# A backward pass on one core: when the first turned pieces of w1 and the row buffer are set up

## The chip, the cores and the metric

The kernel runs on one core of a Trainium2 chip. The metric is the device time of one execution in microseconds; three executions of the kernel before gave 1100.77, 1101.2 and 1102.52.

The core has five engines with instruction streams of their own: PE (TensorE, matrix products; its weight loads are listed as PEld), DVE (VectorE), ACT (ScalarE), POOL (GpSimd) and SP (SyncE, which only issues loads here). Semaphores order them. Data comes from HBM into SBUF by DMA transfers.

## The reference

Two rows (a batch of 2, one token each, width 1024) go through attention, an MLP, the same attention and the same MLP again, each with a layer norm ahead of it and added to the residual. The kernel returns the result and the gradients of everything in it for a given gradient of the output.

```python
x = x + A(layernorm(x), k_cache, v_cache, wq, wo)   # layer 0: 32 heads, 4 KV heads, 16384 keys, width 128
x = x + B(layernorm(x), w1, b1, w2, b2)             # 1024 -> 3584 -> 1024, gelu
x = x + A(layernorm(x), k_cache, v_cache, wq, wo)   # layer 1: the same weights and caches
x = x + B(layernorm(x), w1, b1, w2, b2)
# returned: x, and by vjp with grad_out the gradients of x, k_cache, v_cache, wq, wo, w1, b1, w2, b2
```

The caches are 33.6 MB each for K and V, and they are read from HBM in every attention, forward and backward, but for some pieces that are kept from one pass to the next. The gradients that are written have the size of what they belong to.

## The kernel before, in words

**A program of steps, and a planner.** The kernel doesn't issue instructions as it is read. `emit(fn, uses)` (L71) appends a step to a list; `uses` names the chunks (pieces of data of up to 1 MB, [128, 4096] bfloat16) that the step touches. At the end `Program.run` (L109) goes through the list in order, gives each chunk a home (one of the buffers that the profile calls `slot`, `late`, `e` and `ds`) and calls the steps, which then issue instructions. The order on each engine is thus the order of `emit`.

A chunk with a load is fetched by a DMA on SP's queue (L378 for K and V, L383 for rows of weights). Loads are taken in the order of first use. Before each step the planner hands out homes for the next loads as long as it can: a home must be free, it must not be given up before the chunk's last use, and `possible` (L124) must find that every later chunk still gets a home in time, the chunks without a load (turned copies, the row buffer) included. Of the homes that fit, `fit` takes the one that is given up first. A load whose home was used by others waits, in SP's queue, until their last readers are done; the loads behind it wait too. A chunk without a load gets its home at its first step.

Around the change there are 17 homes of 1 MB. Nine last to the end. Eight are given up for staging outputs later on: three at the mark "late", the others in the course of the next stage (marks 4, 8, 12, 16 and 18, L23 and L24, L1612).

**Turned pieces.** A product with a transposed weight needs the weight turned. For w1, `turn_rows` (L436) does it on DVE: two 32x32 transposes (L442) turn one loaded piece into a turned copy, a chunk of its own, t, which `turned_products` (L484, matmuls at L492) then uses. w1 comes here in eight pieces, 0 to 7 (`ws1c`), of 896 KB; piece 7 is turned already from earlier in the program. So there are 14 turns, `t1[0]` to `t1[13]`, two for each of the pieces 0 to 6, and eight groups of products, `p1[0]` to `p1[7]`. A loaded piece's home is free after its second turn, a turned copy's after its products. w2 was turned in place earlier (`turn_here`) and lies in seven groups, 0 to 6; `here_products` (L466, matmuls at L470) uses it four rows j at a time, 32 matmuls for a group.

**The place of the change** is the passage from the backward attention of layer 1 to that of layer 0. `attn_bwd(1, ...)` (L1048) ends with `after`, then `tail` (the products with the last wq, at L470, eight steps), then `parts` (the layer norm's backward: sums at L672 to L677, closing at L683, rest at L690 to L693, which gives gM_all). Before the change `after` is `t1[0:1]`. Then come: the zeroing of the row buffer Y on ACT (L1533; Y holds rows that the products of weight gradients read later, and lasts to the end), `t1[1:3]`, the products of w2 with gM_all for j = 0 to 27 with one turn behind each of the first three groups, the step `dh0_` (L1543, and the spread at L511 and L512), the mark "late", the step that puts the first rows into Y (`y_rows`, L1300 and L1301), `t1[6:8]`, and the products `p1` with a unit of the weight gradients of w2 (`dw_units`, L1337) and the remaining turns between them:

```python
for n, b in enumerate(p1):
    emit(*b)
    for u in first[n + 1:n + 2] + t1[8 + n + max(0, n - 5):9 + n + max(0, n - 4)]:
        emit(*u)
```

Behind them stands the layer norm's backward of the MLP (L540 to L693), the products with wo (L470), the spread of the result, and the first block of layer 0's attention: `kblock` (L548), which turns a part of a V piece on DVE (L554) and multiplies on PE (L567). Its outputs, the gradients of K and V, are cast by ACT and DVE (L276, L279) and written by POOL's queue (L1287); the weight gradients are written at L1367.

Of the kernel before, what the change touches and what calls it, by code (L numbers as in the profile page):

```python
# [10 lines left out]
I32 = mybir.dt.int32  # L11
# [46 lines left out]
class Program:  # L58
# [12 lines left out]
    def emit(self, fn, uses=()):  # L71
        i = len(self.ops)
        self.ops.append((fn, tuple(uses)))
        for c in uses:
            if c.first is None:
                c.first = i
            c.last = i
# [105 lines left out]
def kernel(  # L183
# [26 lines left out]
    S = nc.scalar  # L210
# [16 lines left out]
    CH = 4096  # L227

    P = Program()
    emit = P.emit  # L230
# [66 lines left out]
    for w in range(2):  # L297
        for e in range(2):
            V.tensor_copy(out=selp[:, 2 * w + e],
                          in_=ident[:].rearrange("p (w t e) -> p w e t", w=2, e=2)[:, w, e].unsqueeze(1).to_broadcast(  # L300
                              [128, 4, 32]))
# [38 lines left out]
    wide = {}  # L340
# [23 lines left out]
    saved = {}  # L364
# [101 lines left out]
    def here_products(c, off, n, ps, v, fresh=True):  # L466

        def fn():
            for o in range(n):
                PE.matmul(ps(), lhsT=c.ap[:, off + o * 128:off + (o + 1) * 128], rhs=v(o),  # L470
                          start=(fresh and o == 0), stop=(o == n - 1), skip_group_check=True)

        return fn, [c]
# [152 lines left out]
    def col_to_row(colT, dram_out, queue=None, kind="half"):  # L626
        c = P.chunk(kind=kind)

        def f():
            row = c.ap[0:DJ, 0:256].rearrange("p (b n) -> p b n", b=2)  # L630
            ps = ob()[0:DJ, 0:256].rearrange("p (b n) -> p b n", b=2)
            for b in range(2):
                PE.transpose(ps[:, b, :], colT[:, :, b], identf[:])
            V.tensor_copy(out=row, in_=ps)
            (queue or GP).dma_start(dram_out.rearrange("b (j n) -> j b n", n=128), row)

        return f, [c]
# [352 lines left out]
    def wo_first_ops(l, k, ws=None):  # L990

        ws = ld_wo(k) if ws is None else ws
        ps = sb[0][:, 64:80].rearrange("p (r b) -> p r b", b=2)
        turns = [turn_here(ws[r // 4], (r % 4) * 1024, 8) for r in range(R)]
        prods = [here_products(ws[r // 4], (r % 4) * 1024, 8, lambda r=r: ps[:, r, :],
                               lambda o: gA_all[:, o, 2 * l:2 * l + 2]) for r in range(R)]
        return ws, turns, prods + [(lambda: do_of(l, k, ps), ())]
# [41 lines left out]
    def wq_last_ops(l, k):  # L1039

        ws = ld_wq(k)
        ps = sb[0][:, 112:128].rearrange("p (j b) -> p j b", b=2)
        turns = [turn_here(ws[j // 4], (j % 4) * 1024, 8, "act" if l == 1 else None) for j in range(DJ)]
        prods = [here_products(ws[j // 4], (j % 4) * 1024, 8, lambda j=j: ps[:, j, :],
                               lambda r: dq_all[:, k * R + r, 2 * l:2 * l + 2], l == 0) for j in range(DJ)]
        return turns, prods

    def attn_bwd(l, order, gT, wo_first, outputs=None, mark=None, extra=None, after=()):  # L1048

        kvs = []  # L1050
        for g in order:
# [40 lines left out]
        for pos, g in enumerate(order):  # L1092
            quick = l == 0 and pos == G - 1
            for f in range(2):
                n = 117 + 5 * f if quick else 16 * pos + 10 + 8 * f
# [9 lines left out]
        tail = []  # L1105
        for i, k in enumerate(kvs):
# [16 lines left out]
            else:  # L1123
                if l == 0:
                    wb.setdefault(32 * i + 12 + LAG_B, []).append((dn_kept, ()))
                ops, tail = wq_last_ops(l, k)
# [11 lines left out]
        while s <= n_steps:  # L1138
# [16 lines left out]
            n = -(-len(fill) // 3)  # L1155
            for fn, us in pre:
                emit(fn, us)
            between = fill[:n] + mids + fill[n:2 * n]
            for v in v_at.get(s, ()):
# [4 lines left out]
                between = []  # L1164
# [9 lines left out]
        aflush()  # L1174
        parts = attn_in_bwd(l, gT, dnq)
        if l == 1:
            todo = list(after) + tail + parts
        else:
            rows, kv_units, units = outputs(s, True)
            todo = ev.pop(s) + kv_units[0:4] + rows + kv_units[4:6] + tail[0:4] + kv_units[6:8] + tail[4:] + kv_units[8:10]  # L1180
            todo += parts[0:1] + units[0:4] + parts[1:2] + units[4:8] + parts[2:3] + kv_units[10:15] + parts[3:]
            todo += kv_units[15:] + units[8:]
# [4 lines left out]
    def attn_in_bwd(l, gT, dnq):  # L1187
        h = {}

        def sums():  # L1190
            last = sb[0][:, 112:128].rearrange("p (j b) -> p j b", b=2)
            if l == 0:
                dn = wrk.tile([128, DJ, 2], F32, name="dn")
                V.tensor_tensor(out=dn[:], in0=last, in1=dnq[:], op=ALU.add)
                last = dn[:]
            h["dr"], h["s"], h["g"] = ln_bwd_terms(last, vec_y[f"a{l}"][:], vec_r[f"a{l}"][:], gT()[:])
            dve(0.8)

        def close():
            h["ps"] = ln_bwd_sums(h["dr"], h["s"], h["g"], half[0, 0] if l == 1 else sb[0][:, 200:])  # L1200

        def rest():
            gn = saved[f"gA{l}"]
            ln_bwd_rest(h["ps"], h["dr"], vec_y[f"a{l}"][:], ([gM_all[:, :, 0:2]] if l == 1 else []) + [gn[:]])
            dve(0.8)

        res = [(sums, ()), (close, ()), (rest, ())]
        if l == 0:
            res.append(col_to_row(saved["gA0"], out_1.rearrange("b s d -> (b s) d"), nc.sync))
        return res  # L1210
# [82 lines left out]
    Y = P.chunk()  # L1293

    def y_rows(colT, j0, jn, q, at_):

        def f():
            tp = ob().bitcast(BF16)[32 * q:32 * q + 4, 0:jn * 128].rearrange("p (a b) -> p a b", b=128)
            for j in range(jn):
                PE.transpose(tp[:, j, :], colT[:, j0 + j, :], ident[:])  # L1300
            S.copy(out=Y.ap[32 * q:32 * q + 4, at_:at_ + jn * 128], in_=flat(tp))  # L1301
            load_of("act", 0.7)

        return f, [Y]
# [105 lines left out]
    up = [b * HKV + k for k in range(HKV) for b in range(2)]  # L1410
# [3 lines left out]
    def mark(name):  # L1414
        def f(n=0):
            marks[name, n] = len(P.ops)
        return f
# [61 lines left out]
    ws_o, wo_turns1, wo_prods = wo_first_ops(1, up[0] % HKV)  # L1479
# [28 lines left out]
    extra = {2: [(lambda: V.memset(fps1, 0.0), ())]}  # L1508
# [13 lines left out]
    t1, p1 = [], []  # L1522
    for n, c in enumerate(ws1c):
        t = w1t[n // 4][n % 4] if n == 7 else P.chunk()
        t1 += [] if n == 7 else turn_rows(c, t, 896)
        p1 += turned_products(lambda n=n: dm_0[:, n // 4], t, 14 * (n % 4), 14, vh0, n % 4 == 0, n % 4 == 3)
    extra[111] = [col_to_row(xM1, out_0.rearrange("b s d -> (b s) d"), kind="load")]
    attn_bwd(1, up, lambda: saved["g3"], (None, wo_prods), mark=mark("d1"), extra=extra, after=t1[0:1])
    wo_prods0 = wo_first_ops(0, down[0] % HKV, saved["wo"])[2]


    g2 = saved["gA1"]
    emit(lambda: S.copy(out=Y.ap.bitcast(I32), in_=wide["n"][:, 0:2].bitcast(I32).to_broadcast([128, CH // 2])), [Y])  # L1533
    for b in t1[1:3]:
        emit(*b)
    for j in range(FJ):
        emit(*here_products(ws2c[j // 4], (j % 4) * 1024, 8, lambda j=j: dhps0[:, j, :],
                            lambda o: gM_all[:, o, 0:2]))
        if j % 4 == 3 and j < 12:
            emit(*t1[3 + j // 4])  # L1540

    def dh0_():
        V.scalar_tensor_tensor(out=dh_all[:, :, 0:2], in0=dhps0, scalar=-1.0, in1=saved["nslope0"][:], op0=ALU.mult,  # L1543
# [6 lines left out]
    emit(lambda: load_of("dve", 6.0))  # L1550
    first = [y_rows(gM_all, 0, 8, 0, 0)] + dw_units("h", 0, 0, pieces_rows(out_8, F, D))
    rest_h = first[15:]
    for b in first[0:1] + t1[6:8]:
        emit(*b)
    for n, b in enumerate(p1):
        emit(*b)
# [10 lines left out]
    extra = {4: [(spread_a0, ())]}  # L1567
# [22 lines left out]
    def outputs(s, rest=False):  # L1590
        if rest:
            fin = late.pop(s)
            return fin[0:1], sum([sched.pop(x) for x in sorted(sched)], []), bg + fin[1:]
        if s in STAGE:
            mark(s)()
        if s in (68, 78):
            mark("done")(s // 78)
        res = list(sched.pop(s, ()))
        if s in late:
            bg.extend(late.pop(s))  # L1600
        if s >= 5:
            state["credit"] += 0.5 if s < 24 else max(1.3, len(bg) / (120 - s)) if s < 116 else 3
        while bg and state["credit"] >= 1:
            res.append(bg.pop(0))
            state["credit"] -= 1
        state["credit"] = min(state["credit"], 2.0)
        return res

    attn_bwd(0, down, lambda: saved["g1"], (va0, wo_prods0), outputs=outputs, extra=extra)
    slots = []  # L1610
    for i, t in enumerate(slot_tiles):
# [46 lines left out]
```

## Time and profile before

| | |
|---|---|
| median of 3 runs | 1101.2 us (1100.77 to 1102.52) |
| the profiled execution | 1101.63 us, span 1099.9 us, mean granted PE clock 0.829 |
| busy: PE, PEld, DVE, ACT, POOL | 820.7, 609.9, 753.9, 487.3, 176.3 us |
| DMA | 448.07 MB, 407 GB/s over the span |
| HBM | 347.23 MB read, 98.62 MB written |

The span runs from the first to the last instruction of the program; the execution's time has a little more around it. The profile also gives the busy share of the 16 DMA engines and the clock that PE was granted, in any stretch. In the rows of the timeline the columns are start, duration, engine, line, operation, what it writes and reads, shapes, how many, and in brackets how long the engine was idle ahead of it and what ended that. A row can merge several instructions of one kind that follow each other; for SP its duration is from the first issue to the last.

### The profile page before, as it was taken

The page shows a single profiled execution, that of the slowest core. Times are in us where ns is not written, and L with a number is a line of the kernel's source. Part 1 is how long each engine was busy: PE and PEld are TensorE (multiplying, and loading weights), DVE is VectorE, ACT ScalarE, POOL GpSimd, SP SyncE. Part 2 cuts the span into 40 slices and gives each one's busy share as a digit, 9 for nine tenths or more (in the row PEclk, how much of TensorE's full clock was granted, in tenths as well). Part 3 has the DMA queues.
Part 4 walks back from the last instruction along what each step waited for, and adds up shares of the span by engine and source line. Part 5 has one row for each costly group of instructions (what it writes and reads, how often), then busy time and mean ns, then how long its engine had stood idle before and what let it go on. Part 6 is the DMA issues. An engine that isn't in the chain of part 4 may idle for free. (4 is left out here: it accounts for less than half of the span.)

```text
span 1099.9 us, 34167 instructions
## 1 busy us (share of the span) xinstructions
PE 820.7 (75%) x14717; PEld 609.9 (55%) x14717; DVE 753.9 (69%) x1442; ACT 487.3 (44%) x1101; POOL 176.3 (16%) x550
## 2 busy tenths in 40 slices
PE   5665666457788657788877678988787788887886
PEld 4554565456777547687877574544443344443453
DVE  5864665168888727765745465978786779786985
ACT  0332222101242321235534326777675667675874
POOL 1000000001000000111211111332332333333330
PEclk9999999999555555579767757989997899898998
DMA  9999999999999999999999999999999999999996
GB/s 368 420 423 420 421 425 422 398 394 408 419 421 421 421 422 378 413 418 420 416 422 403 367 362 415 357 422 423 420 402 425 422 420 415 424 422 422 414 423 269
DMA packets 97404, 448.07 MB, mean 407 GB/s; under 512 B 7608, under 2 KB 11214, under 8 KB 58852
## 3 DMA queue, kind: packets, MB, share of 16 engines
q1 hardware_dynamic: 80004, 350.40, 78.3%
q0 software_dynamic: 17248, 95.48, 21.0%
q8 instruction: 115, 1.88, 0.6%
q14 instruction: 37, 0.30, 0.1%
HBM read 347.23 MB, written 98.62 MB: 405 GB/s over the span
## 5 line engine op out<-in xcount | busy, mean ns | idle before, releaser
L554 DVE STREAM_TRANSPOSE kT<-slot 128x512 int32<-128x512 int32 x432 | 291.7, 695 | 114.5 <-PE sc L567 91.3
L567 PE MATMUL sc<-qbd,kT 128*128 128x32 bf16 x4096 | 263.8, 223 | 13.0 <-DVE kT L554 10.3
L567 PEld LDWEIGHTS <-kT 128*128 128x128 bf16 x4096 | 209.1, 115 | 53.4 <-issue 21.7
L592 PEld LDWEIGHTS <-slot 128*128 128x128 bf16 x3424 | 141.0, 103 | 105.8 <-issue 54.9
L276 ACT CAST slot<-sc 128x512 bf16<-128x512 f32 x294 | 167.3, 592 | 65.2 <-PE sc L1337 29.8
L592 PE MATMUL sb<-xt,slot 128*128 128x8 bf16 x3424 | 156.8, 177 | 41.8 <-DMA slot<-in_A_v_cache_dram 24.1
L1277 PE MATMUL sc<-slot,late 128*128 128x512 bf16 x358 | 135.6, 403 | 29.7 <-DVE slot L279 11.5
L279 DVE CAST slot<-sc 128x512 bf16<-128x512 f32 x163 | 109.3, 677 | 35.8 <-PE sc L1277 15.5
L787 ACT ACTIVATE e<-sc 128x512 bf16<-128x512 f32 x32 | 19.0, 597 | 235.3 <-DVE sc L784 168.5
L460 ACT COPY slot<-tp 128x512 int32<-128x512 int32 x92 | 52.5, 586 | 113.8 <-PE tp L457 93.5
L276 ACT CAST slot<-sb 128x512 bf16<-128x512 f32 x135 | 80.1, 593 | 33.5 <-PE sb L1277 12.5
L457 PE MATMUL tp<-ident,slot 128*128 128x128 bf16 x800 | 75.7, 256 | 14.0 <-DMA slot<-in_A_wq_dram 8.1
L1277 PEld LDWEIGHTS <-late 128*128 128x128 bf16 x512 | 44.4, 99 | 63.6 <-issue 51.2
L602 ACT COPY xt<-e 32x128 int32<-32x128 int32 x256 | 75.6, 295 | 3.9
L1277 PE MATMUL sb<-slot,late 128*128 128x512 bf16 x154 | 62.5, 406 | 16.6 <-ACT slot L276 5.9
L279 DVE CAST slot<-sb 128x512 bf16<-128x512 f32 x92 | 62.5, 679 | 16.5 <-PE sb L1277 7.6
L457 PEld LDWEIGHTS <-slot 128*128 128x128 bf16 x800 | 61.3, 117 | 17.0 <-DMA slot<-in_A_wq_dram 8.5
L1337 PE MATMUL sc<-slot,late 128*128 128x512 bf16 x151 | 60.5, 419 | 4.2 <-DVE slot L279 1.5
L602 POOL COPY xt<-ds 32x64 int32<-32x64 int32 x128 | 29.5, 231 | 180.6 <-DVE ds L1070 107.1
L602 POOL COPY xt<-late 32x64 int32<-32x64 int32 x240 | 55.2, 230 | 15.0 <-DVE late L1070 2.3
L662 POOL TENSOR_TENSOR m_rstd<-ln_vpe,neghalf 128x2 f32<-128x2 f32 x2 | 1.4, 718 | 349.5 <-DVE ln_vpe L660 349.5
L442 DVE STREAM_TRANSPOSE slot<-slot 128x1024 int32<-128x1024 int32 (+1 forms) x44 | 50.9, 1182 | 1.0 <-DMA slot<-in_B_w_dram 0.9
(291 smaller groups left out, 1083.3 us busy)
## 6 DMA issues: line engine op xcount, KB each, us to landing
slot<-in_A_k_cache_dram SPq DMA_DIRECT2D x102, 1024.0 KB, 15.4
slot<-in_A_v_cache_dram SPq DMA_DIRECT2D x100, 1024.0 KB, 17.0
out_dram<-slot POOLq DMA_DIRECT2D x55, 1024.0 KB, 15.8
slot<-in_A_wq_dram SPq DMA_DIRECT2D x26, 1024.0 KB, 15.5
slot<-in_A_wo_dram SPq DMA_DIRECT2D x25, 1024.0 KB, 18.3
out_dram<-slot POOLq DMA_DIRECT2D x40, 512.0 KB, 16.6
slot<-in_B_w_dram SPq DMA_DIRECT2D x21, 896.0 KB, 15.7
slot<-in_B_w_dram SPq DMA_DIRECT2D x12, 1024.0 KB, 13.4
```

The source lines that it names most:

```text
L276: S.copy(out=dst, in_=src)
L279: V.tensor_copy(out=dst, in_=src)
L442: V.transpose(out=t.ap[:, h * nw * 256:(h + 1) * nw * 256].bitcast(I32).rearrange("p (w j m) -> p w j m", j=4, m=32), in_=c.ap[:, 0:4 * nc ...
L457: PE.transpose(tp[:, j * 128:(j + 1) * 128], c.ap[:, off + j * 128:off + (j + 1) * 128], ident[:])
L460: S.copy(out=d.bitcast(I32), in_=tp.bitcast(I32))
L554: V.transpose(out=kT[:].bitcast(I32).rearrange("p (w j m) -> p w j m", w=4, j=4), in_=c.ap[:, (i % 4) * 1024:(i % 4 + 1) * 1024].bitcast(I ...
L567: PE.matmul(sc[:, a0:a0 + 4, :, 2 * (i % 4) + q], lhsT=kv[:, 2 * q + w, :, e], rhs=qbd[:, q_at(g), 2 * w + e], start=(w == 0 and e == 0), ...
L592: PE.matmul(acc, lhsT=c.ap[:, n * 128:(n + 1) * 128], rhs=xv[:, i // 4, t // 2, :, 2 * (i % 4) + t % 2], start=(fresh and i == 0 and t == ...
L602: (GP.tensor_copy if on[t % len(on)] == "g" else S.copy)(out=d[32 * t:32 * t + 32, c0:c0 + cn, j, :], in_=s[32 * j:32 * j + 32, c0:c0 + cn ...
L787: S.activation(out=e_of(l, g)[:, 8 * f:8 * f + 8].rearrange("p a h b -> p h a b"), in_=sc[f][:].rearrange("p h (a b) -> p h a b", b=8), fu ...
L1277: PE.matmul(ps, lhsT=hold["blk"][:, j, :], rhs=flat(qm(w)[:, hf * 4:hf * 4 + 4, :]), start=True, stop=True)
L1337: PE.matmul(ps, lhsT=hold[j // 4 * 4][:, j % 4, :], rhs=Y.ap[:, y_at + c0:y_at + c0 + cn], start=True, stop=True)
```

## The change

Only the order of steps changes. The first turn leaves the end of `attn_bwd(1, ...)`, and the parameter `after` goes with it. The zeroing of Y and the first turns stand behind groups of w2's products: both turns of piece 0 behind group 0, the zeroing and the first turn of piece 1 behind group 1, the second turn of piece 1 behind group 2, the first of piece 2 behind group 3. The second turn of piece 2 moves behind `dh0_` and the step of Y's first rows, ahead of the two turns of piece 3.

```diff
-    def attn_bwd(l, order, gT, wo_first, outputs=None, mark=None, extra=None, after=()):
+    def attn_bwd(l, order, gT, wo_first, outputs=None, mark=None, extra=None):
...
         if l == 1:
-            todo = list(after) + tail + parts
+            todo = tail + parts
...
-    attn_bwd(1, up, lambda: saved["g3"], (None, wo_prods), mark=mark("d1"), extra=extra, after=t1[0:1])
+    attn_bwd(1, up, lambda: saved["g3"], (None, wo_prods), mark=mark("d1"), extra=extra)
...
     g2 = saved["gA1"]
-    emit(lambda: S.copy(out=Y.ap.bitcast(I32), in_=wide["n"][:, 0:2].bitcast(I32).to_broadcast([128, CH // 2])), [Y])
-    for b in t1[1:3]:
-        emit(*b)
+    zero_y = (lambda: S.copy(out=Y.ap.bitcast(I32), in_=wide["n"][:, 0:2].bitcast(I32).to_broadcast([128, CH // 2])), [Y])
+    between = {3: t1[0:2], 7: [zero_y] + t1[2:3], 11: t1[3:4], 15: t1[4:5]}
     for j in range(FJ):
         emit(*here_products(ws2c[j // 4], (j % 4) * 1024, 8, lambda j=j: dhps0[:, j, :],
                             lambda o: gM_all[:, o, 0:2]))
-        if j % 4 == 3 and j < 12:
-            emit(*t1[3 + j // 4])
+        for b in between.get(j, ()):
+            emit(*b)
...
-    for b in first[0:1] + t1[6:8]:
+    for b in first[0:1] + t1[5:8]:
         emit(*b)
```

## The prediction

> **What bounds the kernel now.** I read the profile page first. Its slices of DMA load and traffic say that the transfers set the pace nearly everywhere: some 420 GB/s in most of the 40 slices, with few dips.
>
> ```profile
> DMA  9999999999999999999999999999999999999996
> GB/s 368 420 423 420 421 425 422 398 394 408 419 421 421 421 422 378 413 418 420 416 422 403 367 362 415 357 422 423 420 402 425 422 420 415 424 422 422 414 423 269
> ```
>
> One slice is 27.5 us, so the change lies in slice 24 (632 to 660 us) and the 357 of slice 26 follows it. Busy time by stretches of 2 us shows what is lost at the change (columns: PE, PEld, DVE, ACT, POOL busy; granted clock; DMA share; GB/s):
>
> ```profile
> 646.00:648.00 2.00, 2.00 (x81) 2.00 (x79) 1.56 (x2) 0.00 (x0) 0.29 (x1) 0.50 0.25 92
> 648.00:650.00 2.00, 1.53 (x30) 1.33 (x28) 0.73 (x2) 0.00 (x0) 0.00 (x0) 0.50 0.65 113
> ```
>
> Against 423 GB/s this hole lacks (331 + 310) x 2 us = 1.28 MB, or 3.0 us. The timeline of SP's queue shows its cause: the queue takes its loads in order, and after 639.92 none leaves until 647.59, when piece 5 of w1 goes.
>
> ```profile
> 633.15 15.35 SPq L383 DMA_DIRECT2D slot<-in_B_w_dram  x5
> 648.60 5.18 SPq L378 DMA_DIRECT2D slot<-in_A_v_cache_dram  x4
> 684.53 0.38 SPq L383 DMA_DIRECT2D slot<-in_A_wo_dram  x1
> 693.31 0.33 SPq L378 DMA_DIRECT2D slot<-in_A_v_cache_dram  x1
> ```
>
> Piece 5 waits for the home of piece 2, which the sixth turn leaves. The next hole is what decides. In stretches of 5 us:
>
> ```profile
> 685.00:690.00 5.00, 3.83 (x32) 1.67 (x30) 4.34 (x8) 3.22 (x7) 2.93 (x13) 1.00 0.99 359
> 690.00:695.00 5.00, 4.83 (x68) 2.92 (x68) 4.27 (x8) 3.66 (x8) 1.80 (x3) 1.00 0.84 321
> 695.00:700.00 5.00, 4.78 (x49) 2.39 (x48) 4.62 (x8) 4.22 (x9) 0.00 (x0) 1.00 0.95 264
> ```
>
> It lacks (64 + 102 + 159) x 5 = 1.63 MB, 3.8 us. Here the loads wait for computing: those at 684.53 and 693.31 wait for homes that the V turns of the next stage (L554) leave. From 669 to 725 us the waits of DVE name only PE, never a DMA. So between the two holes computing sets the time; from 700 to 1060 the DMA share stays at 1.0 or above, and a delay reaching 700 stays in the end.
>
> What starts that computing is DVE's order:
>
> ```profile
> 642.33 1.10 DVE L442 STREAM_TRANSPOSE slot<-slot 128x896 int32<-128x896 int32 x1
> 643.47 2.10 DVE L442 STREAM_TRANSPOSE slot<-late 128x896 int32<-128x896 int32 x2
> 645.50 2.06 DVE L442 STREAM_TRANSPOSE slot<-slot 128x896 int32<-128x896 int32 x2
> 648.84 0.22 DVE L1543 SCALAR_TENSOR_TENSOR dh_all<-sb,nslope 128x56 bf16<-128x56 f32 x1 [1.28 <-PE sb L470]
> 649.49 1.09 DVE L512 TENSOR_TENSOR kT<-sb,quad 128x896 bf16<-128x896 f32 x1 [0.43 <-PE sb L511]
> 650.49 8.36 DVE L442 STREAM_TRANSPOSE slot<-slot 128x896 int32<-128x896 int32 x8
> 661.55 0.23 DVE L540 TENSOR_TENSOR uq<-sb,quad 128x64 f32<-128x64 f32 x1 [2.70 <-PE sb L492]
> ```
>
> Eight turns stand back to back; the last products of w1 wait for the last turn at 658.85, and everything up to the first V turn at 668.96 is one chain behind them.
>
> **The change part by part.** Nothing is added or removed but order: 14 turns, one zeroing, the same loads.
>
> Turn 0 leaves its place ahead of the sums of the layer norm. There it ran 639.43 to 640.54, while the sums needed products that PE ended at 640.44. Taking it away gives at most 0.1 us; I take 0.
>
> Turns 0 to 4 now stand among the products of w2. PE starts these at 642.38 and does 224 in 6.4 us, 28.7 ns each. By the planner's rule the homes are: turned piece 0, the second half of wq (free since 640.4); the row buffer, the home of w2 group 0; turned piece 1, piece 0's own; turned piece 2, w2 group 3's, free after 128 products at 646.05. Groups 1 and 2 leave homes that are given up at "late" and serve nobody. DVE is free from 642.4, so turns 0 to 3 end at 646.6 and turn 4 at 647.7. The dh0 step waits for PE until 648.84 as now. This part costs nothing, hidden by the products; without that cover one turn would cost 1.05.
>
> The zeroing (1.90 us at 640.53 on ACT) moves behind 64 products, 644.2. ACT has nothing until 650.48. Ends at 646.1, cost 0; no queue is passed but ACT's, and it issues no DMA.
>
> Turn 5 goes behind dh0. The block of eight becomes nine: 8.36 / 8 = 1.045 us more in front of the last products. Queued behind it on DVE are the turns of pieces 3 to 6, and PE waits for them. Its ends are 0.3 (PE has a 0.75 us pause put down to "issue" among the last products, which a later start may swallow) and 1.1 (one whole turn); below nothing is excluded, since no step of the chain gets shorter. I take 1.05, because in before PE already waits for the last turn, so each turn there is paid.
>
> Loads, in order on SP. The last K piece's home, until now turned piece 0's, is free at 638.2 and goes to piece 4 (639.56 now, about 638.5 then). Piece 5 gets the first half of wq's home at about 639.6 instead of 647.59. That puts 0.92 MB, 2.17 us at 423 GB/s, into the hole. Piece 6 takes the home of w2 group 4, after 160 products, at 647.0 (648.01 now); the next two V pieces follow at 648 and 649. Bytes came back about 2 us after the issue at 647.59 (113 GB/s in 648 to 650, 402 in the next two), so the hole ends near 649 and shrinks from 3.0 to some 0.8 us.
>
> Then the other side. One lasting home now holds a V piece, and piece 2's home and that of turned piece 5 are too short-lived for what comes next. The V and K loads at 652.62 to 655.31 go 1 to 2 us later, the K at 656.49 waits for the last products (662.4), wo moves from 661.55 to 666.6, and the K at 666.52 waits for the second V piece's turns, now ending at 679.60, then at 680.6. From the load at 684.53 on each home is released by the same step as now. So the 2.17 us gained are used up before 684: the same bytes are there, the engines run out earlier, and the hole of 685 to 700 grows by 2.17 plus the 1.05 of later computing, with a part of it at 677 to 681. None of these pieces is needed before 700, so no engine starves.
>
> The sum: 0 + 0 + 0 + 1.05 from the turn, 0 net from the loads. The profiled execution took 1101.63 (span 1099.9 and 1.7 around it), 0.43 above the median of 1101.2. So 1102.7 for such an execution, 1102.2 as a median.
>
> **The clock as a rule.** PE was granted half its clock from 630 to 675, and full from 674.96, right after a stretch in which it was never idle (cut by 3.41 us, so that the cuts meet the point where the clock opens):
>
> ```profile
> 668.13:671.55 3.42, 2.76 (x18) 1.54 (x20) 2.11 (x5) 1.77 (x4) 0.72 (x1) 0.50 1.00 419
> 671.55:674.96 3.41, 3.41 (x40) 2.23 (x39) 1.76 (x4) 2.08 (x6) 0.00 (x0) 0.50 1.00 380
> 674.96:678.37 3.41, 3.07 (x38) 1.64 (x36) 1.38 (x3) 3.41 (x8) 0.00 (x0) 1.00 1.06 418
> ```
>
> If it is judged in such stretches, computing that comes 1.05 later brings the last idle piece of PE (0.66 us before 670.48) to the edge of the decisive one, and the clock may open one stretch later. At half clock ACT is busy 2.08 of 3.41, at full 3.41 of 3.41, so computing advances at 0.61 of the pace and the stretch costs 3.41 x 0.39 = 1.3 us. The Trainium skill ("TensorE: Matmul & The Clock Gate", Part 1, What's actually happening) states just this against the change: a window of about 3.4 us must be busy before the clock opens. It adds that the window runs free of the kernel; by that its edge lies elsewhere in each execution, and the loss would be a chance, not a rule. 640 to 660, with PE busy 17.4 of 20 at half clock, shows that busy alone does not open it.
>
> **The rivals.**
> *Faster, the hole's gain is kept (0.20).* For it: the transfers are at 1.0 in all but a few stretches, and 3.0 us are idle at the place that is filled. Against it: the next hole waits for computing. It holds if the releases at 684 to 699 come earlier too. Then 2.17 to 3.0 are won: median 1098.2 to 1099.0.
> *Slower, the clock opens one stretch late (0.18).* Place: 671 to 678. Price: 1.05 + 1.3 = 2.4, median 1103.6. It decides once more than a trace of idle PE falls into the stretch that now opens it.
> *Slower, the delayed K megabyte is not made up (0.10).* If the engines find no idle time before 700 to catch up, 1.05 + 2.48 = 3.5: 1104.7. The 3.8 us hole speaks against it.
> *It does not do what it says (0.05).* The planner gives piece 5 no earlier home, since the check that later pieces fit forbids it. Then the hole stays and the turn's 1.05 too: 1102.2.
>
> **How the numbers follow.** The forecast has 0.47 and its own range 1101.3 to 1103.0 (the ends of the turn and the spread of the runs). Within 0.2%, 2.2 us, which is about what a measurement of this kernel can tell from no change, lie the forecast and the last rival: 0.52. Faster 0.20, slower 0.28. The range reaches into the faster rival to 1098.6 and over the clock's to 1104.4.
>
> **What would show it.** Right: piece 5 is issued near 639.6, the traffic of 646 to 650 is above 300 GB/s, nine turns follow L512 to about 659.9, the first V turn starts near 670.0, and the traffic of 677 to 700 is lower than now. Wrong: the first V turn at 669 or earlier, a full clock that opens elsewhere, or 685 to 700 filled.

## The result, and the profile after

The changed kernel took 1105.07 us (median of 7 runs, 1103.77 to 1106.27) beside 1101.86 us for the kernel before (7 runs): a ratio of 1.0028, interval 1.0018 to 1.0037. A second comparison (e1 below) gave 1.0011, interval 1.0000 to 1.0022. Both intervals contain a loss of 2.0 to 2.4 us, so the change costs about 0.2%. The first median lies above the predicted range.

The profiled execution after took 1106.27 us, span 1104.5. It is already 1.84 us late where gM_all is written (644.00 against 642.16). A second profile of the same kernel (e1) is 1.10 us early there (641.06), so this doesn't come from the change. Times below are therefore counted from gM_all where the two are compared. From gM_all to the end of the span: 457.7 us before, 460.5 after, 2.8 more.

The page of after, its slices of DMA load and traffic:

```profile
DMA  9999999999999999999999899999999999999996
GB/s 379 420 423 420 422 425 422 398 386 402 413 423 420 422 420 361 408 417 421 417 421 402 358 392 364 351 422 423 419 415 425 422 420 406 424 422 421 417 424 258
```

Slice 24, where the change lies, rose from 362 to 392 GB/s, and slice 25 fell from 415 to 364: what is moved earlier is missing behind. SP's queue shows the loads themselves:

```profile
635.02 14.02 SPq L383 DMA_DIRECT2D slot<-in_B_w_dram  x5
649.63 9.12 SPq L378 DMA_DIRECT2D slot<-in_A_v_cache_dram  x4
...
683.67 0.33 SPq L378 DMA_DIRECT2D slot<-in_A_k_cache_dram  x1
688.58 0.38 SPq L383 DMA_DIRECT2D slot<-in_A_wo_dram  x1
697.35 0.33 SPq L378 DMA_DIRECT2D slot<-in_A_v_cache_dram  x1
```

The first row ends with piece 6 of w1, near 649; piece 5 ahead of it went at 641.39, 2.61 us before gM_all (before: 5.43 us behind it). The K load that left at 666.52 before is now the one at 683.67. The load ahead of it left at 670.79, and from there on the queue stands still. Busy time by stretches of 2 us (PE, PEld, DVE, ACT, POOL, clock, DMA share, GB/s):

```profile
646.00:648.00 2.00, 2.00 (x77) 1.97 (x75) 1.97 (x3) 1.15 (x1) 0.00 (x0) 0.50 1.05 407
648.00:650.00 2.00, 2.00 (x79) 2.00 (x77) 1.40 (x2) 0.00 (x0) 0.52 (x1) 0.50 1.05 405
650.00:652.00 2.00, 0.10 (x4) 0.04 (x2) 0.00 (x0) 0.00 (x0) 0.00 (x0) 0.50 1.04 368
680.00:685.00 5.00, 4.45 (x53) 2.45 (x53) 3.26 (x6) 4.90 (x11) 0.57 (x1) 1.00 0.56 232
```

The hole in the traffic at 646 to 650 is filled, but in 650 to 652 PE is busy for 0.10 us and no other engine computes, and a new hole stands at 680 to 685 (before: 426 GB/s there). PE's timeline has the idle time. First the kernel before, then after:

```profile
642.38 5.77 PE L470 MATMUL sb<-gM_all,slot 128*128 128x2 bf16 x211 [0.68 <-DVE gM_all L693]
648.31 0.49 PE L470 MATMUL sb<-gM_all,slot 128*128 128x2 bf16 x13 [0.16 <-issue]
```

```profile
644.22 5.88 PE L470 MATMUL sb<-gM_all,slot 128*128 128x2 bf16 x211 [0.68 <-DVE gM_all L693]
652.49 0.49 PE L470 MATMUL sb<-gM_all,slot 128*128 128x2 bf16 x13 [2.38 <-issue]
```

The products of w2 run at nearly the same pace (5.88 us for the first 211, against 5.77), but between product 211 and 212 PE stands for 2.38 us instead of 0.16, and the profile names nothing that it waits for ("issue"). DVE follows:

```profile
653.01 0.21 DVE L1542 SCALAR_TENSOR_TENSOR dh_all<-sb,nslope 128x56 bf16<-128x56 f32 x1 [3.62 <-PE sb L470]
653.66 1.09 DVE L512 TENSOR_TENSOR kT<-sb,quad 128x896 bf16<-128x896 f32 x1 [0.43 <-PE sb L511]
654.67 9.35 DVE L442 STREAM_TRANSPOSE slot<-slot 128x896 int32<-128x896 int32 x9
665.83 0.23 DVE L540 TENSOR_TENSOR uq<-sb,quad 128x64 f32<-128x64 f32 x1 [1.81 <-PE sb L492]
```

Counted from gM_all, dh0 starts 9.01 us on (before 6.68: 2.33 later), the block of turns ends at 20.0 (16.7: 3.3 later), the L540 step comes at 21.8 (19.4: 2.4 later), and the first V turn at 29.2 (26.8: 2.4 later).

What PE may be waiting for shows in a part of the DMA view that the prediction did not use: beside the data there is a queue q8, "instruction", with packets of 16,384 bytes. Before, over 642.6 to 646.0 and then 646.0 to 647.0 (packets, MB, share of the engines):

```profile
q1 hardware_dynamic: 750, 1.30, 99.9%
...
q1 hardware_dynamic: 79, 0.13, 34.5%
q8 instruction: 1, 0.02, 6.2%
```

After, over 644.5 to 650.0 and then 650.0 to 651.0:

```profile
q1 hardware_dynamic: 1266, 2.20, 104.4%
...
q1 hardware_dynamic: 206, 0.35, 104.1%
q8 instruction: 1, 0.02, 5.5%
```

In both, one such packet starts some 0.2 us after gM_all. The next one starts 3.9 us after gM_all before, in the hole, and 6.2 us after gM_all with the hole filled. PE goes on 2.2 and 2.3 us behind it. That is the theory to test: **PE waits for its own instructions, and they come late because the data queue is full.**

### The profile page after: what moved, and what is told of

It reads as the page before. It is cut to its first block, busy times and chain, and to the rows that moved or that the text cites. A ratio compares the mean times of both kernels' runs of the same rounds, so it can differ in the third digit from the quotient of the medians.

```text
span 1104.5 us, 34168 instructions
## 1 busy us (share of the span) xinstructions
PE 816.5 (74%) x14717; PEld 608.9 (55%) x14717; DVE 753.4 (68%) x1442; ACT 486.0 (44%) x1101; POOL 176.3 (16%) x550
```

## The experiments

The rivals to it were the ninth turn in the block, the late K load (both from the prediction), something bound to that place in the program, and a disturbance of one run. Products are counted within the 224 of w2; times are us after gM_all, from one profiled execution each; "to the end" is from gM_all to the end of the span. The ratios come from many executions and weigh more than that column.

| run | pause behind product | 2nd packet | PE goes on | dh0 | first V turn | to the end | ratio to before |
|---|---|---|---|---|---|---|---|
| before | 211 | 3.92 | 6.15 | 6.68 | 26.80 | 457.7 | |
| after | 211 | 6.18 | 8.49 | 9.02 | 29.24 | 460.5 | 1.0028 (1.0018 to 1.0037) |
| e1 after again | 211 | 5.98 | 8.48 | 9.01 | 29.23 | 460.8 | 1.0011 (1.0000 to 1.0022) |
| e2 homes back | 211 | 4.46 | 6.70 | 7.22 | 27.59 | 458.2 | 0.9999 (0.9988 to 1.0010) |
| e3 turn 5 back | 211 | 5.98 | 8.23 | 8.75 | 28.90 | 460.0 | 1.0014 (1.0003 to 1.0024) |
| e4 filler in before | 211 | 6.08 | 8.38 | 8.91 | 28.32 | 459.5 | 1.0012 (1.0001 to 1.0024) |
| e5 half of it | 211 | 5.36 | 7.69 | 8.21 | 27.89 | 458.3 | one run |
| e9 piece 5 held | 211 | 4.19 | 6.49 | 7.01 | 27.20 | 458.8 | 0.9996 (0.9988 to 1.0005) |
| e13 16 products more | 195 | 6.06 | 8.28 | 9.23 | 29.45 | 460.9 | one run |
| e14 64 more | 147 | 6.26 | 8.68 | 10.90 | 31.11 | 462.0 | one run |
| e15 128 more | 83 (and 211) | 6.00 | 8.19 | 12.73 | 32.94 | 464.2 | one run |

**e1: the changed kernel once more**, beside e2, e3 and e4.

> The changed kernel once more, for a second profile. Fetch theory (PE's own instruction fetch comes late when the data queue is full, so PE pauses among the products of w2 with gM_all, L470, which the hole at 646 to 650 us used to prevent): the row of L470 before dh0 shows a pause of 2.0 to 2.6 us put down to issue, dh0 starts 8.7 to 9.2 us after gM_all (6.7 in the kernel before), time +2.5 to +4 us. If the pause was an accident of one execution (turn theory: only the ninth turn costs): pause under 0.5 us and about +1 us.

Same pause (2.49 us), same place, same chain; a disturbance of one execution is out. The time rose less than expected: 1.0011 is 1.2 us, and the interval reaches from 0 to 2.4.

**e2: the order of after, the homes of before.** By steps that only touch them, the first turned pieces and Y take their homes about where they took them before, and are still written where after writes them. So piece 5 of w1 again finds no early home.

```diff
...
-    attn_bwd(1, up, ..., extra=extra)
+    attn_bwd(1, up, ..., extra=extra, after=[(lambda: None, t1[0][1])])
...
+    emit(lambda: None, [Y])
-    between = {3: t1[0:2], 7: [zero_y] + t1[2:3], 11: t1[3:4], 15: t1[4:5]}
+    between = {3: t1[0:2] + [(lambda: None, t1[2][1][1:])], 7: [(lambda: None, t1[4][1][1:]), zero_y] + t1[2:3], ...}
```

> The changed order of turns, but turned piece 0, the row buffer and turned pieces 1 and 2 take their homes where the kernel before gave them, by steps that only touch them. So piece 5 of w1 finds no home before w2's group 3 leaves one (about 3.7 us after gM_all), and the hole in the transfers is back. Fetch theory: the pause among the products falls under 0.6 us, dh0 starts 6.6 to 7.3 us after gM_all, nine turns follow as in the changed kernel, time +0.5 to +1.5 us. Load theory (what costs is that later K, V and wo loads go out later and one lasting home is gone; these are as late here as in the changed kernel): +2.5 to +4 us as in the changed kernel. Turn theory: +1 us.

```profile
648.61 0.48 PE L470 MATMUL sb<-gM_all,slot 128*128 128x2 bf16 x13 [0.70 <-issue]
```

All of the order is kept, nine turns in the block too, and the K load is as late as after (38.4 us after gM_all). The pause shrinks from 2.38 to 0.70 us (expected was under 0.6), and the loss is gone. What costs is not where the turns stand but the load that they let go.

**e3: turn 5 stays among the products,** so the block has eight turns and the hole is filled.

```diff
-    between = {3: t1[0:2], 7: [zero_y] + t1[2:3], 11: t1[3:4], 15: t1[4:5]}
+    between = {3: t1[0:2], 7: [zero_y] + t1[2:3], 11: t1[3:4], 15: t1[4:6]}
...
-    for b in first[0:1] + t1[5:8]:
+    for b in first[0:1] + t1[6:8]:
```

> The changed kernel, but the second turn of piece 2 stands among the products of w2 again (behind group 3, with the first), so eight turns follow L512 and not nine. Loads and homes up to there are those of the changed kernel. Fetch theory: the pause of 2 to 2.6 us stays; the last turn ends 1.0 us sooner counted from dh0, and the layer norm behind the last products starts 0.2 to 1.0 us sooner; time +1.5 to +3 us. Turn theory: all of the loss was the ninth turn, so 0 to +0.5 us.

PE's rows, the pause among w2's products and the largest among the last ones of w1:

```profile
650.05 0.48 PE L470 MATMUL sb<-gM_all,slot 128*128 128x2 bf16 x13 [2.23 <-issue]
...
662.92 0.35 PE L492 MATMUL sb<-kT,slot 128*128 128x8 bf16 x7 [0.92 <-issue]
```

The pause stays, and so does the loss. The first V turn comes 0.34 us sooner than after, but dh0 already comes 0.27 sooner, so the ninth turn costs only 0.1 us here: with one turn less PE meets another pause of "issue", 0.92 us, that the turn otherwise covers.

**e4 and e5: the kernel before with its hole filled by other bytes.** Order, homes and loads are those of before; POOL's queue stores 1 MB (e5: half of it) to an unused tensor from the moment gM_all is there.

```diff
...
+    def fill():
+        GP.tensor_copy(out=dh_last[:, 0, :], in_=gM_all[:, 0, 0:2])
+        GP.dma_start(scr[:], Et[0][:, 0:CH])
+    emit(fill)
```

> The kernel before with its own order and homes, and one more store on POOL's queue: 1 MB of the kept exponentials goes to a scratch buffer in HBM, issued once gM_all is there (about 642.2 us), so that the hole of 646 to 650 us is filled with bytes of no use. Fetch theory: the pause among the products, 0.16 us in before, grows to 1.5 to 2.6 us, dh0 starts 8 to 9.2 us after gM_all, time +1.5 to +4 us. Turn and load theories: no pause (under 0.5 us), dh0 6.7 us after gM_all; the megabyte goes into idle time, so 0 to +1 us.

> As the filler in the kernel before, but with half the bytes: 0.5 MB, 1.24 us of traffic, so a part of the hole is left. Fetch theory: the pause among the products of w2 lies between those without (0.16 us) and with 1 MB (2.39 us), 0.8 to 1.9 us, and the instruction packet that ends it starts between 3.9 and 6.1 us after gM_all. If a filler only disturbs by its presence (POOL's store, a contended bank), the pause is 2.2 to 2.6 us as with 1 MB.

PE in e4, then in e5 (L471 is L470 of the others):

```profile
641.93 5.77 PE L471 MATMUL sb<-gM_all,slot 128*128 128x2 bf16 x211 [0.68 <-DVE gM_all L694]
650.09 0.49 PE L471 MATMUL sb<-gM_all,slot 128*128 128x2 bf16 x13 [2.39 <-issue]
```

```profile
652.34 0.48 PE L471 MATMUL sb<-gM_all,slot 128*128 128x2 bf16 x13 [1.70 <-issue]
```

A store that nothing waits for makes the same pause in the unchanged order (2.39 us, beside 2.38 and 2.49 after). Half the bytes leave 1.70 us of it, with the packet at 5.36 us instead of 6.08. The time of e4 rises by 0.1% (interval 0.01% to 0.24%); e5's one run took 1104.71 beside 1102.81 for before.

**e6 to e8: holding loads back with a tiny store, which went wrong.** In e6 the load of piece 5 stands on SP's queue behind a store of [128, 2] of a turned piece, 4 bytes from each partition; `held` keeps the planner from issuing it sooner. In e7 the next V pieces of the kernel before are held in the same way until the eleventh turn (to give the packets behind a free queue), and e8 adds to e7 one more turn behind w2's group 3.

```diff
...
+    def gate(t, *keys):
+        emit(lambda: nc.sync.dma_start(scr[:], t.ap[:, 0:2]), [t])
+        for k in keys:
+            P.held[k] = len(P.ops)
...
+        if j == 15:
+            gate(t1[4][1][1], ("w1q", 4, 896))
```

> The changed kernel with its own order of turns (nine behind L512); only the load of piece 5 is held in SP's queue by a tiny store of turned piece 2 (its first turn ends 5.4 us after gM_all) ahead of it, so the hole is back where the kernel before had it. Later loads go no earlier than in the changed kernel. Fetch theory: pause under 0.6 us, dh0 6.6 to 7.3 us after gM_all instead of 9.0, time -0.5 to +1 us against before. Load and turn theories: the ninth turn and the late loads are all there, so +1 to +4 us whatever the pause does.

> The kernel before; the loads from the first V piece of the next stage on are held in SP's queue until the first turn of piece 5 is done (about 13.5 us after gM_all; 648.60 before, some 655.7 then), by a tiny store. More hole, less prefetch. Fetch theory: the instruction packets behind dh0 follow each other sooner (6.4 us apart in before, under 5.5 then), the pause of 0.75 us among the last products goes, the layer norm behind them (L540) starts 0.2 to 0.9 us sooner after gM_all than the 19.4 of before; time -1 to +0.3 us. Load theory (every load that goes later costs): +2 us or more.

> The held loads of the run before this one, and the first turn of piece 3 among the products of w2 too (behind group 3), so seven turns follow L512. Fetch theory: with the packets sooner, DVE's turns are what the last products wait for, so one turn less gives up to 1.0 us: L540 starts 17.8 to 18.8 us after gM_all, time -2 to -0.3 us against before. If fetch still sets the pace there, L540 stays at the value of the run before this one and the time too.

They took 1.0072 (1.0058 to 1.0086), 1.0066 (1.0054 to 1.0079) and 1.0051 (1.0039 to 1.0064) of before. The stretches of e6 show why they say nothing about the question:

```profile
650.00:652.00 2.00, 1.14 (x38) 1.02 (x36) 0.22 (x1) 0.00 (x0) 0.00 (x0) 0.50 0.90 41
652.00:654.00 2.00, 1.74 (x29) 1.48 (x29) 1.60 (x2) 0.60 (x1) 0.00 (x0) 0.50 0.49 22
654.00:656.00 2.00, 2.00 (x54) 1.72 (x52) 1.97 (x3) 0.77 (x2) 0.00 (x0) 0.50 0.80 70
```

The DMA engines are 45 to 90% busy and move 22 to 70 GB/s, from 650 to 660. PE then has a pause of 7.28 us. Only the early part can be used: with the hole kept, w2's pause was down to 0.58 us.

**e9: the same as e6 with a store of 16 pieces of 3 KB.** The order and the nine turns are those of after; piece 5 goes at 648.86, 5.7 us after gM_all, by the planner's rules into another home.

```diff
-        emit(lambda: nc.sync.dma_start(scr[:], t.ap[:, 0:2]), [t])
+        emit(lambda: nc.sync.dma_start(scr[:], t.ap[0:16, 0:1536]), [t])
```

> The changed kernel with the load of piece 5 held again, but by a store of 16 partitions x 3 KB (48 KB) in place of the 4-byte pieces, which had kept the transfers busy for some 8 us. Nine turns behind L512, later loads no earlier than in the changed kernel. Fetch theory: pause among the products under 0.6 us, dh0 6.6 to 7.3 us after gM_all (9.0 in the changed kernel), L540 19.4 to 20.6 us after gM_all (21.8), time -0.5 to +1.5 us against before. Load and turn theories: no change against the changed kernel, +1 to +4 us.

Stretches and PE's rows of e9 (L474 is L470 of the others):

```profile
646.00:648.00 2.00, 2.00 (x78) 2.00 (x78) 2.00 (x3) 0.00 (x0) 0.44 (x1) 0.50 0.74 282
648.00:650.00 2.00, 1.81 (x69) 1.75 (x66) 0.45 (x1) 0.00 (x0) 0.09 (x1) 0.50 0.28 64
```

```profile
645.92 3.55 PE L474 MATMUL sb<-gM_all,slot 128*128 128x2 bf16 x128 [0.16 <-issue]
649.67 0.48 PE L474 MATMUL sb<-gM_all,slot 128*128 128x2 bf16 x13 [0.19 <-issue]
```

The hole is back, the pause is 0.19 us, and the time is that of before. The block has nine turns, and the late K load leaves 37.9 us after gM_all instead of 24.4. So with the hole kept, the turn and the late megabyte together cost nothing that can be measured.

**e10 to e12: the V loads of the kernel before held, with the better store.** The idle time of the queue is put where the packets for the last products of w1 start: until the eleventh turn (e10), the same with a turn more among w2's products (e11), until the ninth (e12).

> The kernel before with the loads from the first V piece on held until the first turn of piece 5 is done, by a store of 48 KB. Fetch theory: the third instruction packet behind gM_all starts 13.5 to 15 us after it (16.8 in before), L540 starts 18.2 to 19.0 us after gM_all (19.4), and since the V pieces still land before they are needed, time -1.2 to +0.5 us. Load theory: some 3.5 us of transfers less before 660 us must be paid, +2 us or more.

> The same hold, and the first turn of piece 3 among the products of w2, so seven turns follow L512. Fetch theory with turns as the next limit: L540 17.4 to 18.3 us after gM_all, time -2 to 0 us. If PE's own work is the next limit: L540 as in the run with the hold alone.

> The hold of the V loads ends two turns sooner, at the first turn of piece 4 (about 11.5 us after gM_all), which costs 2 us less of transfers. Fetch theory: the third packet comes between 14 and 16.8 us after gM_all, L540 18.4 to 19.4 us, time -1 to +0.5 us.

Ratios 1.0005 (0.9997 to 1.0014), 1.0007 (0.9997 to 1.0018) and 1.0002 (0.9992 to 1.0011): nothing won. In e10 the L540 step came 0.5 us sooner (18.90 us after gM_all), as expected. In e11 it came at 19.20, where 17.4 to 18.3 was expected. The hole of 685 to 700 is filled (422, 417 and 422 GB/s in its stretches of 5 us), and as much is missing at 656 to 660 (35) and 660 to 665 (321). Moving the hole moves no time.

These runs show one more thing. They keep the hole behind gM_all, and yet the pause among w2's products is 0.71 us in e10, 1.24 in e11 and none in e12. It follows the moment at which the queue runs dry: from 4.0 to 4.5 us after gM_all the DMA share is 0.37 before, 0.73 in e10 and 0.96 in e11, and the second packet starts at 3.92, 4.24 and 4.80.

**e13 to e15: the changed kernel with PE's program shifted.** Products that are overwritten at once are issued just ahead of those of w2: 16, 64 and 128 (2, 8 and 16 groups of eight; 8 in the diff). If the pause belongs to the place, it stays behind product 211; if to the count of PE's instructions, it moves by as many products.

```diff
+    for j in range(8):
+        emit(*here_products(ws2c[j // 4], (j % 4) * 1024, 8, lambda j=j: dhps0[:, j, :], lambda o: ident[:, 0:2]))
```

> The changed kernel with 16 products more on PE, issued just ahead of the products of w2 while PE waits for gM_all (their sums are overwritten by the products that follow). If PE waits for its instructions, and these come in blocks of 128 products: the pause moves from behind product 211 of w2 to behind product 195, is still 1.8 to 2.8 us long, and the second instruction packet after gM_all still starts 2.2 to 2.6 us before PE goes on; dh0 8.7 to 9.5 us after gM_all. If the pause belongs to the place in the program: it stays behind product 211.

> The same with 64 products more (1.8 us, some 0.7 of it in PE's idle time). Instructions: the pause lies behind product 147 of w2, 1.5 to 3 us long; dh0 9.5 to 10.8 us after gM_all. Place: the pause stays behind product 211.

> The same with 128 products more, one whole block (3.7 us). Instructions: a pause behind product 83, and one behind product 211 again, as the place comes round; dh0 11.5 to 14.5 us after gM_all. Place: one pause, behind product 211, and none behind 83.

PE's rows of e13, e14 and e15:

```profile
647.27 3.56 PE L470 MATMUL sb<-gM_all,slot 128*128 128x2 bf16 x128 [0.19 <-issue]
653.21 0.91 PE L470 MATMUL sb<-gM_all,slot 128*128 128x2 bf16 x29 [2.38 <-issue]
```

```profile
647.36 3.55 PE L470 MATMUL sb<-gM_all,slot 128*128 128x2 bf16 x128 [0.70 <-issue]
653.57 2.19 PE L470 MATMUL sb<-gM_all,slot 128*128 128x2 bf16 x77 [2.66 <-issue]
```

```profile
647.85 2.35 PE L470 MATMUL sb<-gM_all,slot 128*128 128x2 bf16 x83
652.58 3.55 PE L470 MATMUL sb<-gM_all,slot 128*128 128x2 bf16 x128 [2.38 <-issue]
656.60 0.48 PE L470 MATMUL sb<-gM_all,slot 128*128 128x2 bf16 x13 [0.47 <-issue]
```

29, 77 and 141 products remain behind the pause, where 13 did: it lies behind product 195, 147 and 83. In e15 the place behind 211 comes round after 128 products more and has a second, small pause, since the transfers had run out by then (the next packet came 3.9 us behind the last, not 6). The pause belongs to PE's instructions, in blocks of 128 products with their weight loads. dh0 of e14 was 0.1 us beyond what was expected, all else within.

## Why the prediction was wrong, and where it was right

**The step that failed** is the part on turns 0 to 4: "The dh0 step waits for PE until 648.84 as now. This part costs nothing, hidden by the products". It took the 6.4 us of the 224 products as fixed, and asked only whether DVE's turns fit under them. They do (the fifth turn ends at 649.4, 3.6 us ahead of dh0). But the cover itself grew: 8.8 us, 2.33 of the 2.44 us by which the first V turn came late. The traffic of 646 to 650 was counted as idle time that filling could only help or leave; it was the gap in which PE's instructions came. No rival had that mechanism.

**The sum.** The V turn's delay goes through to the end: over before, after, e2, e3, e4, e9, e14 and e15 it is 0, 2.4, 0.8, 2.1, 1.5, 0.4, 4.3 and 6.1 us, and the time from gM_all to the end grows by 0, 2.8, 0.4, 2.2, 1.8, 1.1, 4.3 and 6.5. In e1, e5 and e13 it is 2.4, 1.1 and 2.7 beside 3.1, 0.6 and 3.2. So the predicted chain from the block of turns into the end holds, as far as single executions show it; the term in front of it was missing. It doesn't hold where V loads were held: in e10 and e11 the V turn came 0.5 and 0.2 us sooner and the end 1.7 and 2.0 later. By its time alone e1, 1.2 us slower, would have looked like the 1.05 of the forecast; that would have been luck, as its pause is 2.49 us.

**The ninth turn, +1.05.** On DVE it took 1.0 us (9.35 against 8.36). On the chain much of it came back: the 0.75 us pause among the last products, which the prediction named as what "a later start may swallow", was swallowed. From the end of the block to L540 it takes 1.8 us instead of 2.7. From dh0 to L540 it is 12.8 us with nine turns and 12.7 with eight (before and e3), so the price was 0.1, below the end of 0.3 that was given, and not the 1.05 taken. But e4, with eight turns, the same pause among w2's products and none above 0.24 us among the last ones, takes 12.0. Beside it the ninth turn costs 0.8: its price hangs on where PE's next pause falls.

**Turn 0 and the zeroing, 0 each:** right. From the start of the last 64 products ahead of gM_all to gM_all it is 3.57 us in both. The first piece's turns start right behind gM_all, and DVE is idle again before dh0.

**The loads, 0 net:** right for the bytes, early and late; e9 shows that the late ones cost nothing. But the early load of piece 5 is what held up PE's instructions. Piece 5 went at 641.39, or 639.55 once the 1.84 us by which that execution ran late are taken off (predicted 639.6). The traffic of 646 to 650 is 407 and 405 (predicted over 300). In the first 12 us after gM_all the lack of bytes against 423 GB/s shrank from 3.5 to 0.6 us. From 12 to 65 us it grew from 4.2 to 8.8, that is by 4.6, near the sum of the predicted 2.17 for the bytes and 2.44 for the computing that came later. In e1 it grew by 5.3. Of the stated marks, the end of the nine turns was forecast 17.7 us after gM_all and the first V turn 27.8; they came at 20.0 and 29.2.

**The rivals.** *Faster:* refuted; the gain at the hole was given back at 680 to 705. *The clock one stretch late:* not what happened. Full clock came 34.43 us after gM_all, 5.2 behind the first V turn (before 32.80, and 6.0 behind it), so against the work it came sooner. It opened right behind a stretch of 3.41 us with PE never idle, as before. In the other 16 profiles it came 5.2 to 7.4 us behind the first V turn, in no order that goes with the times. The Trainium skill ("TensorE: Matmul & The Clock Gate", Part 1, What's actually happening) says that the window runs free of the kernel; the spread of 2.2 us agrees. *The K megabyte, 1104.7:* its number is nearest the first median, but e9 keeps the late load and loses nothing. *Does not do what it says:* it does, piece 5 found its early home.

The Trainium skill ("Runtime: NRT & Kernel Launch", Instruction fetch mechanics) says that an engine's instructions come by a DMA queue of its own in blocks of 16 KiB, 256 instructions, while the current block runs, and that the cost is mostly hidden. The trace agrees on the block: 16,384 bytes, and the pauses move in steps of 128 products with 128 weight loads. In the whole execution q8 has 115 packets, and PE 14,717 products and as many weight loads, 256 instructions to a packet. Here the cost isn't hidden: 2.38 us. The Trainium skill ("DMA: Bandwidth & Descriptors", Queues, rings and completion order) has each DMA engine take turns between its queues packet by packet. The trace fits that in so far as the block gets in at 6.2 us with data still queued; how long a turn lasts, it doesn't show. The packet itself takes 0.9 to 1.0 us with the queue full and in the hole alike (5.5% and 6.2% of 16 engines for 1 us); what differs is when it starts.

**What stays open.** The moment at which PE asks for a block isn't in the records, so the wait of a block in the queue is inferred: from the start of the packets, from e4, e5, e2 and e9, which set it by data alone, and from e13 to e15. Why it is some 6 us with a full queue, wasn't tried further. The two comparisons of the same kernel (0.28% and 0.11%) meet only at 2.0 to 2.4 us, and the executions of one kernel spread by more than the effect (e1: 1102.56 to 1108.24 us).

## What to carry to other kernels

A hole in the transfers isn't free room: where PE issues small products densely (28.7 ns each, a block of 128 in 3.7 us), its instruction packets may be what uses it. Look at the instruction queue in the DMA view and at rows that end in "issue" before you fill a hole, and count the cover (here the 6.4 us of the products) as something that the change can lengthen. If a term of the sum is hidden by other work, ask what that work needs from the resource that the change loads.

## What the runs showed of the hardware

- PE's instructions share the DMA engines with the data. Dense products use a block in 3.7 us. The second packet came 5.9 to 6.0 us behind the first with a full queue (after, e1, e3, e4, e13 to e15) and 3.4 to 4.6 us with the hole (before, e2, e6 to e12), about when the queue ran dry; with the full queue PE stood for 2.2 to 2.7 us. In each run with a pause there it went on 2.2 to 2.5 us after the packet's start.
- A store of 512 bytes in 128 pieces of 4 bytes, ahead of the loads on SP's queue, went with 10 us of traffic at 22 to 70 GB/s (e6); 48 KB in 16 pieces of 3 KB did not (e9). The Trainium skill ("DMA: Bandwidth & Descriptors", Specifications) asks for at least 512 bytes in a transfer for the full rate, with a read-modify-write below that. The trace agrees that this store was slow and doesn't show why.
